# One score fill moved from the long visit to the short one, two gate factors loaded earlier, another deal in the first quad

## The chip, the cores and the metric

The kernel runs on one core of a Trainium2 chip. The metric is the device time of one execution in microseconds; the kernel before took 1105.04 us (median of three runs, 1104.69 to 1105.52). Both kernels compute the same.

## The reference, cut to what matters

The input x has 2048 rows of 640. One branch is causal attention in four segments of 512 rows with 32 heads of 20, mixed per head with a linear memory of the earlier segments; the other is a gated feed-forward layer of width 1728. A gate per row mixes them.

```python
g = sigmoid((x * gate_w).sum(-1, keepdims=True))
for s in range(4):                       # segments of 512 rows
    p = softmax(qs @ ks.T * scale + causal_mask)
    a_dot = p @ vs
    a_mem = (phi(qs) @ M) / (phi(qs) @ z + 1e-6)
    o = sigmoid(beta) * a_mem + (1 - sigmoid(beta)) * a_dot
    M, z = M + phi(ks).T @ vs, z + phi(ks).sum()
a = concat(o) @ wo
b = (silu(x @ w1) * (x @ w3)) @ w2
out = g * a + (1 - g) * b
```

## The kernel before

**Dense work.** The four segments are chunks 0 to 3, in two halves A (chunks 0, 1) and B (2, 3). Every 32-bit operand is split into a rounded part and a rest, and each product is three matmuls. A dense group is one PSUM bank of 128 x 512 that is filled by 15 matmuls (`g` and `u`: the two feed-forward projections; `q`, `k`, `v`; `op`: the output projection) or by 9 or 5 (`f`: the second feed-forward product). DVE or ACT then empties it: a `u` group by one DVE pass (`ft`, L528), a `g` group by an ACT pass and a DVE pass (`ft` L519, `fu` L520), an `f` group by a DVE pass (L588, L550) or, in the first group of a chunk, by an ACT copy (L586). Dense work is a list of generators (`seg`), from which `step` draws some three matmuls at a time.

**Banks.** PSUM has eight banks that `bank_tile` deals in rotation from the list `free`. The bank of an open dense group is held back (`held`) and goes to the end of the list when the group's last matmul is issued (`filled`).

**Attention.** Four heads are a quad `m`; each quad is 40 slots of `attention()`. `s_fill` (scores, scanned on DVE for the row maximum, L641), `t_fill` (transposed scores with the maximum subtracted, exponentiated on ACT, L673, cut to a triangle on POOL, L677) and `pv_quad` (`o`, the product with V, copied by DVE, L691) are issued in two visits per quad: the long one at slot `BIG` (5), the short one at slot `SMALL` (17). Each fill has two tiles, one for each of two heads that PE works side by side on different rows of its array; `o` has one tile. The table `VISITS` gives the order: the long visit holds s fill 0 of quad m, t fills 0 and 1 of quad m-1, o of quad m-2, t fill 3, s fill 2, t fill 2 and s fill 1, 15 tiles in all; the short one s fill 3, t fill 4 and s fill 4, six tiles. The visit of quad 1 is cut in two parts: 3 fills, then 4, and 3 in the short visit. A long visit waits until no dense group is open (at most 8 steps), a short one stands also inside an open group. `load_pair` loads the q and k rows of the next quad behind each visit, through POOL's queue.

**Other tiles of the rotation.** The memory read (`nd`, L352), the normalization of the attention output (`rr` and `gt`, L761 and L766, emptied by DVE at L762 and L767), and the split of an input chunk (`xh`, L131) also take banks. Each chunk's sum is multiplied by its gate factor `sh`, which `load_share` loads through ACT's queue (L740); `finish` and `share` use it (L550, L543).

**Order.** PE runs in the order in which the program issues. The order on the other engines is fixed when the kernel is built, by a planner that places each instruction where its inputs are due; each engine then works strictly in that order.

Of the kernel before, what the change touches and what calls it, by code (L numbers as in the profile page):

```python
# [25 lines left out]
BIG = -1.0e38  # L26
# [12 lines left out]
def gated_mix(ctx: ExitStack, tc: tile.TileContext, xT, wqk, wv, w13, w2, w2h, wo, beta, out):  # L39
# [60 lines left out]


    here = tc.keep_in_program_order
    last = {}

    def split(dst, src, lo=None, pin=lambda ins: ins):
        pin(nc.scalar.copy(dst[:, 0], src))  # L106
# [4 lines left out]
    def bank_tile(name, hold=None):  # L111


        k = free.pop(0)
        ps = pp.tile([P, L], F32, tag=f"b{k}", name=name, bufs=1)
        if hold:
            held[k] = -hold
        else:
            free.append(k)
        return ps  # L120
# [6 lines left out]
    def split_psum(dst, src, name, pin=lambda ins: ins):  # L127

        hi = bank_tile(name)[:, :src.shape[-1]]
        pin(nc.scalar.copy(dst[:, 0], src))  # L130
        nc.scalar.copy(hi, dst[:, 0].bitcast(F32))  # L131
        nc.vector.tensor_sub(dst[:, 1], src, hi)
# [134 lines left out]
    late, stored = [], set()  # L267
# [70 lines left out]
    def memory_read(c):  # L338
        pq = big.pop(("q", c))[:, :KB * L].rearrange("p (b n) -> p b n", b=KB)
        for qb in range(4):  # L340
            for hf in range(2):
                gm = f_tile(f"gm{c}_{qb}_{hf}")[:, :320]
                ps = bank_tile(f"nd{c}_{qb}_{hf}")
                nd = ps[:, :16 * VE].rearrange("p (h e) -> p h e", e=VE)
                todo = []
                for b in range(KB):
                    a0, a1 = HEADS[b]
                    u0, u1 = max(a0, 16 * hf), min(a1, 16 * hf + 15)
                    if u0 <= u1:
                        todo.append((b, a0, u0, u1))  # L350
                for n, (b, a0, u0, u1) in enumerate(todo):
                    nc.tensor.matmul(nd[:, u0 - 16 * hf:u1 - 16 * hf + 1, :],  # L352
                                     pq[:, b, qb * P:(qb + 1) * P],
                                     Ms[c - 1, b][:, u0 - a0:u1 - a0 + 1, :],
                                     start=n == 0, stop=n == len(todo) - 1, skip_group_check=True)
                r = sp.tile([P, 16], F32, tag="r16", name="nd_r")
                nc.vector.scalar_tensor_tensor(r, nd[:, :, DH], 1e-6, gH[:, 16 * hf:16 * hf + 16], op0=ALU.add, op1=ALU.mult)
                nc.vector.reciprocal(r, r)
                nc.vector.scalar_tensor_tensor(
                    gm.rearrange("p (h e) -> p h e", e=DH), nd[:, :, :DH], gate[:, c, 1, qb:qb + 1],  # L360
                    r.unsqueeze(2).broadcast_to([P, 16, DH]), op0=ALU.mult, op1=ALU.mult)
                store_later(gd[c][:, qb, 320 * hf:320 * hf + 320], gm, ("g", c, qb), n=2)
                yield 700
# [200 lines left out]
    def ffn_down(cs, js, idx, last=()):  # L564
        first = js[0] == 0
        w2s = [w_get(i, idx[0]) for i in idx]
        for c in cs:
            if c in last and c < 2:
                load_share(c)
            if first:  # L570
                accs[c] = slot(f"acc{c}")[:, :KB * L].rearrange("p (b n) -> p b n", b=KB)
            for fb in range(KB):
                for n0, n1 in ((0, 256), (256, L)) if last and (c, fb) == (NSEG - 1, KB - 1) else ((0, L),):
                    ps = bank_tile(f"f{c}_{js[0]}_{fb}_{n0}", 1300 if len(js) > 2 else 690)
                    ms = []
                    for j, w in zip(js, w2s):
                        for a, b in (PASSES if j < NF else ((0, 0), (0, 1))):
                            ms.append((w[:, b, fb * P:(fb + 1) * P], hts[c, j][:, a, n0:n1]))
                    for n, (w, h) in enumerate(ms):
                        nc.tensor.matmul(ps[:, :n1 - n0], w, h, start=n == 0, stop=n == len(ms) - 1)  # L580
                        if n % 3 == 2 and n < len(ms) - 1:
                            yield 699.0 if n == 2 and len(ms) > 5 else 699
                    filled()
                    dst = accs[c][:, fb]
                    if first:
                        nc.scalar.copy(dst, ps)  # L586
                    elif c not in last:
                        nc.vector.tensor_add(dst, ps, dst)  # L588
                    elif c < 2:
                        finish(c, fb, ps)  # L590
                    else:
                        finish_shared(c, fb, ps, n0, n1 - n0)
                    yield 699 if len(ms) % 3 == 0 else 466

    def both_shares():
        for c in B:
            load_share(c)
            yield 1

# [138 lines left out]
    def load_share(c):  # L738
        shares[c] = sp.tile([P, L], F32, tag="oq" if c == NSEG - 1 else "share", name=f"sh{c}", bufs=1)
        here(nc.scalar.dma_start(shares[c], ed[c][0].rearrange("a n -> (a n)").unsqueeze(0).broadcast_to([P, L])))  # L740
# [12 lines left out]
    def normalize(c):  # L753

        assert c in turned
        if not c:
            gms[c] = big_tile(f"oT{c}", FR)[:, :KB * L].rearrange("p (b n) -> p b n", b=KB)
        for b in range(KB):
            o, hi = f_tile(f"on{c}_{b}"), gms[c][:, b]
            ps = bank_tile(f"rr{c}_{b}")  # L760
            nc.tensor.matmul(ps, sel[:, b * P:(b + 1) * P], rR, start=True, stop=True)  # L761
            nc.vector.tensor_mul(o, oall[c][:, b].bitcast(F32), ps)  # L762
            if c:
                pt = bank_tile(f"gt{c}_{b}")
                for qb in range(4):
                    nc.tensor.transpose(pt[:, qb * P:(qb + 1) * P], hi[:, qb * P:(qb + 1) * P].bitcast(F32), ident)  # L766
                nc.vector.tensor_add(o, o, pt)  # L767
            nc.scalar.copy(hi, o)
            nc.vector.tensor_sub(oall[c][:, b], o, hi.bitcast(F32))
            yield 700  # L770
# [8 lines left out]
    def tick():  # L779
        for e in list(soon):  # L780
            e[0] -= 1
            if e[0] <= 0:
# [4 lines left out]


    BIG, SMALL = 5, 17
    VISITS = {BIG: (("s", 0, 0), ("t", 1, 0), ("t", 1, 1), ("o", 2), ("t", 1, 3), ("s", 0, 2), ("t", 1, 2), ("s", 0, 1)),  # L790
              SMALL: (("s", 0, 3), ("t", 1, 4), ("s", 0, 4))}

    def attention():

        for m in range(-1, NQUAD + 2):
            for n in range(40):
                if m == -1 and n < 40 - LEAD:
                    continue

                todo = VISITS.get(n, ()) if m != 1 else {BIG: VISITS[BIG][:3], BIG + 6: VISITS[BIG][4:]}.get(n, VISITS.get(n, ()))  # L800
                todo = [(kind, m - q, f) for kind, q, *f in todo if 0 <= m - q < NQUAD]
                if todo:
                    yield "amid" if len(todo) < 4 else "between"
                    for kind, q, f in todo:
                        if kind == "o":
                            pv_quad(2 * q)
                        else:
                            (s_fill if kind == "s" else t_fill)(q, *f)
                    if n == SMALL and 0 <= m < NQUAD:
                        after(4, max_rows, 2 * m)  # L810
                elif n in ((24, 36) if m < 0 else (BIG + (1 if m > 1 else 7), SMALL + 1)) and m + 1 < NQUAD:
                    load_pair(2 * (m + 1) + (n > BIG + 7 if m >= 0 else n > 24))
                tick()
                yield m
# [5 lines left out]
    def oproj(c, plan):  # L820

        ws, oT = [], []

        def first():
            yield from normalize(c)
            oT.extend((gms[c], oall[c]))

        def rest():
            ws.extend(w_get(i, plan[0]) for i in plan)
            if c == 1:  # L830
                load_share(c)
            for fb in range(KB):
                ps = bank_tile(f"op{c}_{fb}", 1300)
                n = 0
# [95 lines left out]
    seg = [d, braid(chain(u), o1, 5), o2] + [job_up(A, j) for j in GROUPS[3][2:]] + [job_down(A, 3)]  # L930
    u0, u1 = jobs_up_by_chunk(A, 4)
    x2, x3 = split_x(2), split_x(3)
    seg += [(0, load_raw(2)), (0, load_raw(3))] + u0 + [braid(chain(u1), (0, x2), 4, 0, False)]
    d = job_down(A, 4, (0,))
    q = job_q(B[:1], 0, {2: big_tile})
    seg += [braid(chain([braid(d, (0, x2), 5)] + q), (0, x3), 4, 10)] + job_v(B)
# [21 lines left out]
    segs.append((NJ + LAG, seg))  # L958
    d, u = job_down(B, 3), jobs_up(B, 4)
    o1, o2 = jobs_oproj(3)  # L960
    tail = [braid(chain([d, (0, both_shares())] + u), o1, 4, 10)] + [braid(o2, (0, shared(2)), 3), job_down(B, 4, B)]

    for n, (_, g) in enumerate(head):
        for _ in g:
# [29 lines left out]
    while run:  # L994
# [6 lines left out]
        place = next(att, None)  # L1001
        if isinstance(place, str):

            for _ in range(4 if place == "amid" else 8):
                if (max(held.values(), default=-1) >= 0) if place == "amid" else not held:
                    break
                d = step(run)
                if d is None:
                    break
                credit -= d  # L1010
            next(att)
# [68 lines left out]
```

## Time and profile before

| what | value |
|---|---|
| median of the runs | 1105.04 us |
| the profiled execution | 1107.25 us, span 1105.4 us |
| PE busy | 1094.9 us (99%) |
| DVE, POOL, ACT busy | 598.1, 584.6, 381.3 us |
| granted clock of PE | 1.00 |

A profile row of the timeline gives the start and length in us, the engine, the line, the operation with its tile names, the count, and in brackets the idle time of the engine before it with what ended it. Matmuls overlap: the next starts before the last one has ended, so the time of a stretch is read from start to start.

### The profile page before, as it was taken

Reading aid. Unit: us, or ns where it says so; the run is one execution under the profiler, and the core shown is the slowest. Engines: PE = TensorE matmul, PEld = TensorE weight load, DVE = VectorE, ACT = ScalarE, POOL = GpSimd, SP = SyncE. Lnnn points to the kernel's source line nnn. Section 1 sums busy time; section 2 is a strip of 40 time slices with the busy share of each in tenths; the row PEclk is TensorE's granted clock in tenths of the full one; section 3 lists DMA queues with packets and bytes.
Section 4 is the critical chain, followed back from the end, with each engine's and each line's share of the span. In section 5 each row is a group of like instructions: output and inputs, shape, how many; then the busy total and the mean of one; then the engine's idle time right before and its main releaser. Section 6 shows DMA issues by size and latency. Waiting matters only on the chain.

```text
span 1105.4 us, 17904 instructions
## 1 busy us (share of the span) xinstructions
PE 1094.9 (99%) x6290; PEld 853.0 (77%) x6290; DVE 598.1 (54%) x1711; ACT 381.3 (34%) x826; POOL 584.6 (53%) x729
## 2 busy tenths in 40 slices
PE   9999999999999999999999999999999999999998
PEld 6988877777777777787977777777777777777787
DVE  5032564356555554366153678875557665651575
ACT  6244233343233122145244543325333332223020
POOL 5055556366366363565066447556774665655263
PEclk9999999999999999999999999999999999999999
DMA  8256943334355134435367966365664343433122
GB/s 306 110 205 220 281 125 82 95 82 116 77 142 129 51 84 123 126 94 171 121 197 265 288 215 183 97 161 146 151 159 109 85 116 96 117 103 89 52 79 95
DMA packets 87545, 153.20 MB, mean 139 GB/s; under 512 B 11584, under 2 KB 25184, under 8 KB 87456
## 3 DMA queue, kind: packets, MB, share of 16 engines
q1 hardware_dynamic: 63040, 106.30, 30.1%
q0 software_dynamic: 20384, 38.68, 15.9%
q10 hardware_dynamic: 4032, 7.08, 1.8%
q8 instruction: 50, 0.82, 0.3%
q14 instruction: 39, 0.32, 0.1%
HBM read 96.56 MB, written 54.54 MB: 137 GB/s over the span
## 4 chain that ended last, share of the span: by engine, by line
PE 93%; DVE 4%; ACT 1%; DMA 1%; issue 1%; ACTq 0%; SPq 0%; DVEq 0%
PE g L257 16%; PE f L580 16%; PE u L257 16%; PE k L257 6%; PE v L385 6%; PE op L837 6%; PE o L687 6%; PE q L257 5%; PE s L634 5%; PE t L667 4%; PE nd L352 1%; PE pm L449 1%; PE q L327 1%; DVE junk L641 1%; DMA sh<-ed 1%
## 5 line engine op out<-in xcount | busy, mean ns | idle before, releaser
L641 DVE CUSTOM_DVE_ANT_0 junk<-s,mask 128x256 bf16<-128x256 f32 (+3 forms) x512 | 250.3, 489 | 105.9 <-PE s L634 73.6
L673 ACT ACTIVATE P<-t 128x512 f32<-128x512 f32 (+1 forms) x384 | 172.5, 536 | 190.2 <-PE t L667 153.0
L257 PE MATMUL g<-X,W 128*128 128x512 f32 x840 | 208.5, 398 | 0.0
L179 POOL TENSOR_TENSOR W<-wr,W 128x640 fp32r<-128x640 f32 (+1 forms) x126 | 198.5, 1581 | 2.5
L174 POOL CAST W<-wr 128x640 fp32r<-128x640 f32 (+1 forms) x126 | 92.5, 739 | 202.0 <-PE f L580 47.7
L580 PE MATMUL f<-ht,W 128*128 128x512 f32 (+1 forms) x825 | 197.0, 395 | 0.7 <-DVE acc L550 0.7
L257 PE MATMUL u<-X,W 128*128 128x512 f32 x780 | 196.7, 399 | 0.0
L677 POOL TENSOR_SCALAR_AFFINE_SELECT P<-P 128x256 f32<-128x256 f32 x192 | 94.6, 502 | 183.2 <-ACT P L673 182.9
L257 PEld LDWEIGHTS g<-X,W 128*128 128x128 f32 x840 | 155.9, 188 | 36.6 <-issue 0.4
L580 PEld LDWEIGHTS f<-ht,W 128*128 128x128 f32 x825 | 152.9, 188 | 37.6 <-DVE acc L550 1.5
L257 PEld LDWEIGHTS u<-X,W 128*128 128x128 f32 x780 | 144.0, 188 | 34.4 <-ACT P L673 0.3
L107 POOL TENSOR_TENSOR ht<-ft,ht 128x512 fp32r<-128x512 f32 x52 | 67.2, 1291 | 90.1 <-ACT ht L106 90.0
L611 POOL DMA_DIRECT2D qk<-qkd x128 | 83.6, 655 | 0.5 <-issue 0.2
L634 PE MATMUL s<-qk 60*128 60x256 f32 (+3 forms) x512 | 77.8, 345 | 1.1 <-DVE fu L520 1.0
L257 PE MATMUL k<-X,W 128*128 128x512 f32 x300 | 77.0, 403 | 0.0
L687 PE MATMUL o<-P,vg 128*32 128x512 f32 (+3 forms) x1024 | 75.5, 435 | 1.4 <-DVE on L767 1.4
L519 ACT ACTIVATE ft<-g 128x512 f32<-128x512 f32 x52 | 31.2, 599 | 124.9 <-PE g L257 113.8
L385 PE MATMUL v<-W,X 128*128 128x320 f32 (+1 forms) x480 | 71.9, 311 | 0.3 <-ACT P L673 0.3
L520 DVE SCALAR_TENSOR_TENSOR fu<-ft,g 128x512 f32<-128x512 f32 x52 | 35.7, 686 | 67.3 <-ACT ft L519 58.3
L385 PEld LDWEIGHTS v<-W,X 128*128 128x128 f32 x480 | 71.0, 189 | 1.0 <-ACT P L673 0.5
L106 ACT CAST ht<-ft 128x512 fp32r<-128x512 f32 x52 | 32.2, 619 | 110.9 <-DVE ft L528 110.8
L588 DVE TENSOR_TENSOR acc<-f,acc 128x512 f32<-128x512 f32 x65 | 44.7, 689 | 44.8 <-PE f L580 44.6
(123 smaller groups left out, 1204.8 us busy)
## 6 DMA issues: line engine op xcount, KB each, us to landing
qk<-qkd POOLq DMA_DIRECT2D x128, 240.0 KB, 4.0
wr<-in_w_dram SPq DMA_DIRECT2D x80, 320.0 KB
qkd<-qs SPq DMA_DIRECT2D x20, 512.0 KB
qkd<-ks SPq DMA_DIRECT2D x20, 512.0 KB
od<-oq SPq DMA_DIRECT2D x32, 256.0 KB
wr<-in_wo_dram SPq DMA_DIRECT2D x20, 320.0 KB
vg<-vd SPq DMA_DIRECT2D x16, 336.0 KB
xr<-in_xT_dram SPq DMA_DIRECT2D x20, 256.0 KB
```

The lines of the kernel that those rows point to most:

```text
L107: (lo or nc.gpsimd.tensor_sub)(dst[:, 1], src, dst[:, 0].bitcast(F32))
L174: hi = nc.gpsimd.tensor_copy(w[:, 0, :n], raw[:, :n])
L179: last["low"] = nc.gpsimd.tensor_sub(w[:, 1, :n], raw[:, :n], w[:, 0, :n].bitcast(F32))
L257: nc.tensor.matmul(ps, w[:, a, kb * P:(kb + 1) * P], x[:, b, kb, :], start=n == 0, stop=n == 14)
L385: nc.tensor.matmul(ps[:, :n1 - n0], x[:, a, kb, lb * P:(lb + 1) * P], wvt[kb][:, b, n0:n1], start=n == 0, stop=n == 14)
L580: nc.tensor.matmul(ps[:, :n1 - n0], w, h, start=n == 0, stop=n == len(ms) - 1)
L611: here(nc.gpsimd.dma_start(t[64 * i:64 * i + RH], qkd[c][RH * (h + i):RH * (h + i + 1)]))
L634: nc.tensor.matmul(ps[i][:, o:o + w], q[:, qb * P:(qb + 1) * P], key[:, :w], start=n == 0, stop=n == len(todo) - 1, skip_group_check=True)
L641: nc.vector.tensor_tensor_reduce(out=junk[:, :w], in0=ps[i][:, o:o + w], in1=mask[:, L - w:], scale=1.0, scalar=-3.0e38, op0=ALU.add, op1= ...
L673: last["exp"] = nc.scalar.activation(pairs[2 * m + k]["P"][:, i, o:o + n], ps[i][:, b:b + n], AF.Exp, scale=SCALE)
L677: nc.gpsimd.affine_select(d, d, pattern=[[0, 2], [0, n], [1, P]], base=0, channel_multiplier=-1, compare_op=ALU.is_ge, fill=0.0)
L687: nc.tensor.matmul(ps[32 * i:32 * i + 32, kb * P:], heads[2 * p + i]["v"][:, kb], pairs[p + i // 2]["P"][:, i % 2, o:o + n], start=kb == 0 ...
```

## The change

- A long visit leaves out t fill 3 of quad m-1 when the dense group that was opened last is a `u`, `f`, `op` or `g` group and more than six steps have passed since a small tile took a bank. Then the short visit of that quad has four fills, t fill 3 first (eight tiles), and does not stand inside an open group: from slot 8 on it is taken as soon as the last group is a finished `u`, `f` or `op` group, at least five steps after the long visit and three after the last small tile. At slot 17 it waits for that for up to eight steps, or until 14 steps have passed since the long visit.
- The visit of quad 1 is cut into 4, 3 and 3 fills.
- The gate factor of chunk 0 is loaded ahead of the last feed-forward unit's up projections instead of inside its down projection; that of chunk 1 at the start of the normalization instead of the output projection.

```diff
     def split_psum(dst, src, name, pin=lambda ins: ins):
+        if src.shape[-1] == L:
+            last["small"] = clock["step"]
...
     def ffn_down(cs, js, idx, last=()):
         for c in cs:
-            if c in last and c < 2:
-                load_share(c)
...
+    PLAIN = "ufo"
     VISITS = {BIG: (("s", 0, 0), ("t", 1, 0), ("t", 1, 1), ("o", 2), ("t", 1, 3), ("s", 0, 2), ("t", 1, 2), ("s", 0, 1)),
-              SMALL: (("s", 0, 3), ("t", 1, 4), ("s", 0, 4))}
+              SMALL: (("s", 0, 3), ("t", 1, 4), ("s", 0, 4)),
+              "four": (("t", 1, 3), ("s", 0, 3), ("t", 1, 4), ("s", 0, 4))}
...
-                todo = VISITS.get(n, ()) if m != 1 else {BIG: VISITS[BIG][:3], BIG + 6: VISITS[BIG][4:]}.get(n, VISITS.get(n, ()))
+                todo = VISITS.get(n, ()) if m != 1 else {BIG: VISITS[BIG][:3] + VISITS[BIG][4:5], BIG + 6: VISITS[BIG][5:]}.get(n, VISITS.get(n, ()))
+                if n == SMALL or four and not done and 8 <= n < SMALL:
+                    if not done and 0 <= m <= NQUAD:
+                        yield "amid" if not four else "late" if n == SMALL else "early"
+                        if n == SMALL or last["go"]:
+                            visit(m, VISITS["four" if four else SMALL])
+                            done = True
...
+                    if ("t", 1, 3) in todo and 0 < m <= NQUAD and last["dense"] in PLAIN + "g" and clock["step"] - last["small"] > 6:
+                        four = True
+                        todo = [t for t in todo if t != ("t", 1, 3)]
...
         def first():
+            if c == 1:
+                load_share(c)
             yield from normalize(c)
         def rest():
             ws.extend(w_get(i, plan[0]) for i in plan)
-            if c == 1:
-                load_share(c)
...
-    seg += [(0, load_raw(2)), (0, load_raw(3))] + u0 + [braid(chain(u1), (0, x2), 4, 0, False)]
+    seg += [(0, load_raw(2)), (0, load_raw(3)), (0, load_shares(A[:1]))] + u0 + [braid(chain(u1), (0, x2), 4, 0, False)]
...
+            def ready():
+                if place == "amid":
+                    return max(held.values(), default=-1) >= 0
+                if place == "between":
+                    return not held
+                return not held and last["dense"] in PLAIN and clock["step"] - last["visit"] >= 5 \
+                    and clock["step"] - last["small"] > 2
+            last["go"] = ready()
-            for _ in range(4 if place == "amid" else 8):
-                if (max(held.values(), default=-1) >= 0) if place == "amid" else not held:
+            for _ in range({"amid": 4, "early": 0}.get(place, 8)):
+                if ready() or place == "late" and clock["step"] - last["visit"] >= 14:
                     break
```

More of the change, by code (lines that the diff above doesn't have):

```diff
@@ L102, in gated_mix @@
     here = tc.keep_in_program_order
-    last = {}
+    last = dict(small=0, visit=0)
     def split(dst, src, lo=None, pin=lambda ins: ins):
@@ L117, in bank_tile @@
             held[k] = -hold
+            last["dense"] = name[0]
         else:
@@ L343, in memory_read @@
                 ps = bank_tile(f"nd{c}_{qb}_{hf}")
+                last["small"] = clock["step"]
                 nd = ps[:, :16 * VE].rearrange("p (h e) -> p h e", e=VE)
@@ L593, in ffn_down, with load_shares @@
                     yield 699 if len(ms) % 3 == 0 else 466
-    def both_shares():
-        for c in B:
+    def load_shares(cs):
+        for c in cs:
             load_share(c)
@@ L760, in normalize @@
             ps = bank_tile(f"rr{c}_{b}")
+            last["small"] = clock["step"]
             nc.tensor.matmul(ps, sel[:, b * P:(b + 1) * P], rR, start=True, stop=True)
@@ L789, in gated_mix, with visit @@
     BIG, SMALL = 5, 17
+    PLAIN = "ufo"
     VISITS = {BIG: (("s", 0, 0), ("t", 1, 0), ("t", 1, 1), ("o", 2), ("t", 1, 3), ("s", 0, 2), ("t", 1, 2), ("s", 0, 1)),
-              SMALL: (("s", 0, 3), ("t", 1, 4), ("s", 0, 4))}
+              SMALL: (("s", 0, 3), ("t", 1, 4), ("s", 0, 4)),
+              "four": (("t", 1, 3), ("s", 0, 3), ("t", 1, 4), ("s", 0, 4))}
     def attention():
+        def visit(m, todo):
+            for kind, q, *f in todo:
+                if 0 <= m - q < NQUAD:
+                    if kind == "o":
+                        pv_quad(2 * (m - q))
+                    else:
+                        (s_fill if kind == "s" else t_fill)(m - q, *f)
         for m in range(-1, NQUAD + 2):
+            four = done = False
             for n in range(40):
@@ L798, in attention @@
                     continue
-                todo = VISITS.get(n, ()) if m != 1 else {BIG: VISITS[BIG][:3], BIG + 6: VISITS[BIG][4:]}.get(n, VISITS.get(n, ()))
[L801 to L811, printed above, removed]
+                todo = VISITS.get(n, ()) if m != 1 else {BIG: VISITS[BIG][:3] + VISITS[BIG][4:5], BIG + 6: VISITS[BIG][5:]}.get(n, VISITS.get(n, ()))
+                n_fills = sum(0 <= m - q < NQUAD for _, q, *_ in todo)
+                if n == SMALL or four and not done and 8 <= n < SMALL:
[4 more added lines that the diff above has]
+                            done = True
+                            if m < NQUAD:
+                                after(4, max_rows, 2 * m)
+                elif n_fills:
+                    yield "amid" if n_fills < 4 else "between"
+                    if ("t", 1, 3) in todo and 0 < m <= NQUAD and last["dense"] in PLAIN + "g" and clock["step"] - last["small"] > 6:
+                        four = True
+                        todo = [t for t in todo if t != ("t", 1, 3)]
+                    visit(m, todo)
+                    last["visit"] = clock["step"]
+                if n in ((24, 36) if m < 0 else (BIG + (1 if m > 1 else 7), SMALL + 1)) and m + 1 < NQUAD:
                     load_pair(2 * (m + 1) + (n > BIG + 7 if m >= 0 else n > 24))
@@ L960, in gated_mix @@
     o1, o2 = jobs_oproj(3)
-    tail = [braid(chain([d, (0, both_shares())] + u), o1, 4, 10)] + [braid(o2, (0, shared(2)), 3), job_down(B, 4, B)]
+    tail = [braid(chain([d, (0, load_shares(B))] + u), o1, 4, 10)] + [braid(o2, (0, shared(2)), 3), job_down(B, 4, B)]
     for n, (_, g) in enumerate(head):
```

## The prediction

> **What bounds the kernel now.** I read the page first, then the waits of PE, then the timeline at the places where a wait ended late.
>
> ```profile
> span 1105.4 us, 17904 instructions
> PE 1094.9 (99%) x6290; PEld 853.0 (77%) x6290; DVE 598.1 (54%) x1711; ACT 381.3 (34%) x826; POOL 584.6 (53%) x729
> PE 93%; DVE 4%; ACT 1%; DMA 1%; issue 1%; ACTq 0%; SPq 0%; DVEq 0%
> PE o L687 <- DVE on L767: 1.4, 1, 1.4
> ```
>
> PE is busy for 99% of the span and carries 93% of the chain. The change adds and removes no matmul, so it can only move waits and slow restarts of PE. The last row is the longest wait that PE shows as idle time (total, times, longest); others are hidden inside busy time. The timeline of one quad shows such a one, in columns of start, length, engine, line, operation, count and idle time before:
>
> ```profile
> 318.44 0.50 PE L634 MATMUL s<-qk 60*128 60x512 f32 x2
> 318.78 0.64 PE L667 MATMUL t<-qk 62*128 62x512 f32 x6
> 319.35 2.36 PE L687 MATMUL o<-P,vg 128*32 128x512 f32 x32
> 321.64 0.50 PE L667 MATMUL t<-qk 62*128 62x512 f32 x2
> 321.78 0.69 DVE L691 COPY oq<-o 128x512 f32<-128x512 f32 x1 [0.90 <-PE o L687]
> 321.98 0.40 PE L634 MATMUL s<-qk 60*128 60x512 f32 x2
> 322.21 0.40 PE L667 MATMUL t<-qk 62*128 62x256 f32 x4
> 322.23 2.19 ACT L673 ACTIVATE P<-t 128x512 f32<-128x512 f32 x6 [0.90 <-PE t L667]
> 322.45 0.58 PE L634 MATMUL s<-qk 60*128 60x384 f32 x4
> 322.95 3.77 PE L257 MATMUL u<-X,W 128*128 128x512 f32 x15
> 326.56 1.54 PE L257 MATMUL g<-X,W 128*128 128x512 f32 x6
> 326.76 0.69 DVE L528 SCALAR_TENSOR_TENSOR ft<-fu,u 128x512 f32<-128x512 f32 x1 [0.73 <-PE u L257]
> 328.04 0.51 PE L634 MATMUL s<-qk 60*128 60x256 f32 x4
> 328.38 0.41 PE L667 MATMUL t<-qk 62*128 62x384 f32 x4
> 328.61 0.46 PE L634 MATMUL s<-qk 60*128 60x384 f32 x4
> 329.00 0.96 PE L257 MATMUL g<-X,W 128*128 128x512 f32 x3
> ```
>
> From start to start the long visit takes 4.51 us (318.44 to 322.95), the short one 0.96. A fill of one 512 pair takes 0.34 when it comes first after another kind of work (321.64 to 321.98, 318.44 to 318.78) and 0.23 behind its like (321.98 to 322.21): about 0.10 goes to the switch. The pairs of 384 and 128 take 0.23 as a t fill (328.38 to 328.61); before dense work, 0.10 more, so 0.33. The long visit's last s fill has the same pairs and takes 0.50. It is the 14th and 15th tile on eight banks: the 15th has the bank of o, which DVE copies until 322.47. A matmul starts 0.05 after such a release (below: 154.67 and 154.72), so the second head starts at 322.52 instead of 322.45. A wait of 0.07 costs 0.17, since the two heads no longer run side by side.
>
> **The change part by part.** Term C, the moved fill. On PE, in the long visit of an earlier quad (o is the product with V, t_3 the moved fill, s_2 the next fill; _0 and _1 are the two heads, the last number is a tile's own), before:
>
> ```order
> L687 MATMUL o_2291<-P_2050,vg_93 32x128 x2
> L667 MATMUL t_3_0_2311<-qk_91 128x512
> L667 MATMUL t_3_1_2312<-qk_91 128x512
> L634 MATMUL s_2_0_2319<-qk_90 128x512
> L634 MATMUL s_2_1_2320<-qk_90 128x512
> ```
>
> and in the same quad's short visit of the changed kernel, behind the u group:
>
> ```order
> L260 MATMUL u_3_2369<-X_105,W_1933 128x512 x15
> L669 MATMUL t_3_0_2393<-qk_91 128x512
> L669 MATMUL t_3_1_2394<-qk_91 128x512
> L636 MATMUL s_3_0_2400<-qk_90 128x256
> L636 MATMUL s_3_1_2401<-qk_90 128x256
> ```
>
> The fill now follows a finished u group instead of o. Switches stay as many: s now pays the 0.10 behind o, t pays it behind u, s_3 no longer. The long visit has 13 tiles, so none reuses o's bank: 0.17 saved. By the order this holds for 21 quads with such a last s fill: 21 x 0.17 = 3.57.
>
> The short visit pays. It has eight tiles, and the eighth has the bank of the group just finished. A u group is released 0.73 after its modelled end (322.95 + 3.77 = 326.72; DVE ends at 327.45), plus 0.05; a visit starts 0.08 before that end. So the bank is free 0.86 after the visit's start, wanted at 0.34 + 0.24 + 0.23 = 0.81. That wait of 0.05 costs up to 0.15 with the lost pairing. The next group also takes t_3's bank: the first exponential starts 0.59 after its fill (321.64, 322.23), an ACT pass takes 0.59 (next row), free at 1.23 where 1.20 is wanted: 0.03 at least.
>
> ```profile
> L586 ACT COPY acc<-f 128x512 f32<-128x512 f32 x20 | 11.7, 588 | 23.2 <-PE f L580 18.9 <-DMA qk<-mr 2.2 <-issue 1.7
> ```
>
> Between 0.03 and 0.15 I take 0.09, for 18 visits: 1.62. Two visits follow an f group that ACT copies itself; the exponential then starts late: about 0.15 each, 0.30. One visit (t_3 of quad 11) stands inside an open group, which leaves seven banks: its last tile waits for t_3's own bank (1.23 instead of 0.81), with the pairing 0.5. C = 3.57 - 1.62 - 0.30 - 0.5 = 1.15 gained, between 0.1 and 1.9.
>
> The Trainium skill, TensorEngine Tiling (Array Packing), section Tiling Modes, says that tiles operate independently and load weights and multiply in parallel. By it a late head would cost only its wait, C would be 21 x 0.07 - 18 x 0.05 - 0.8 = -0.2, and the time 1101.4. The trace disagrees: 0.50 against 0.33 for a wait of 0.07.
>
> With the fill go its two exponentials on ACT and one triangle select on POOL, and POOL issues the next pair's loads behind that select:
>
> ```profile
> qk<-qkd POOLq DMA_DIRECT2D x128, 240.0 KB, 4.0
> ```
>
> They land 4.0 us after issue. Until the next long visit's s_2, which needs them, lie at least two dense groups (3.6 each, as 322.95 to 326.56) and 3.5 us of that visit (318.44 to 321.98), 10.7 in all. I cost this at nothing; where the cover is gone, each us late is a us of PE.
>
> Term A, the factor of the first chunk. On ACT before (X and xh: the split of the next input):
>
> ```order
> L130 CAST X_4932<-xr_4776 128x512
> L131 COPY xh_1_4961<-X_4932 128x512
> L131 COPY xh_2_4983<-X_4932 128x512
> L106 CAST ht_12_4971<-ft_12_4972 128x512
> L740 DMA sh_4999<-ed_84 128x512
> ```
>
> and now:
>
> ```order
> L675 ACTIVATE P_4733<-t_2_0_4729 128x256
> L675 ACTIVATE P_4686<-t_2_1_4730 128x256
> L675 ACTIVATE P_4733<-t_2_1_4730 128x256
> L742 DMA sh_4783<-ed_84 128x512
> L535 ACTIVATE ft_13_4812<-g_13_4785 64x512
> ```
>
> The load has moved up by a whole unit, to behind the exponentials of the long visit near 470 us. What it stands in now:
>
> ```profile
> 496.37 0.32 ACTq L740 DMA_DIRECT2D sh<-ed  x1
> 499.76 5.01 PE L580 MATMUL f<-ht,W 128*128 128x512 f32 x21
> 503.12 1.29 DVE L543 TENSOR_TENSOR acc<-acc,sh 128x512 f32<-128x512 f32 x2 [3.35 <-DMA sh<-ed]
> 505.07 1.44 PE L580 MATMUL f<-ht,W 128*128 128x512 f32 x5 [0.30 <-DVE acc L550]
> 506.87 1.43 PE L580 MATMUL f<-ht,W 128*128 128x512 f32 x5 [0.35 <-DVE acc L550]
> 508.67 3.74 PE L257 MATMUL q<-X,W 128*128 128x512 f32 x15 [0.36 <-DVE acc L588]
> 512.34 0.51 PE L634 MATMUL s<-qk 60*128 60x512 f32 x2
> 517.85 2.33 PE L385 MATMUL v<-W,X 128*128 128x320 f32 x14 [0.30 <-ACT P L673]
> ```
>
> Issued at 496.37, it lands near 503; DVE stands 3.35 us with all accumulations queued behind. PE needs 8.91 us (499.76 to 508.67) for 31 matmuls; at the pace of 322.95 to 326.56 (3.61 for 15 with one switch, 0.234 each) it would be 7.25: 1.66 lost. The visit at 512.34 takes 5.51 instead of 4.51: 1.00 more. What is late next is DVE itself: per group of five matmuls (1.17 us) it owes three passes of about 0.64 (1.29 for two), so it still falls behind by 0.7 a group, but the banks cover four groups. I keep 0.2 at the visit: A = 2.45, between 1.0 and 2.66. The issue costs ACT's queue 0.32 under a dense group.
>
> Term B, the second chunk's normalization (rr and gt: its two banks per block). On DVE the order changes from
>
> ```order
> L762 TENSOR_TENSOR on_2_7298<-oall_6264,rr_2_7299 128x512
> L528 SCALAR_TENSOR_TENSOR ft_2_7269<-fu_2_7270,u_2_7273 128x512
> L641 ISA junk,m_7138<-s_0_0_7316,mask 128x512
> L641 ISA m_7138 128x1
> L767 TENSOR_TENSOR on_2_7298<-on_2_7298,gt_2_7302 128x512
> ```
>
> to
>
> ```order
> L765 TENSOR_TENSOR on_2_7300<-oall_6264,rr_2_7301 128x512
> L772 TENSOR_TENSOR oall_6264<-on_1_7279,gm_6764 128x512
> L770 TENSOR_TENSOR on_2_7300<-on_2_7300,gt_2_7304 128x512
> L532 SCALAR_TENSOR_TENSOR ft_2_7271<-fu_2_7272,u_2_7275 128x512
> L643 ISA junk,m_7131<-s_0_0_7318,mask 128x512
> ```
>
> The pass that frees gt_2's bank moves ahead of the u group's and of the first scan. It matters here:
>
> ```profile
> 696.52 1.07 ACTq L655 DMA_DIRECT2D qk<-mr  x2
> 698.45 0.69 DVE L769 TENSOR_TENSOR oall<-on,gm 128x512 fp32r<-128x512 f32 x1 [1.24 <-ACT gm L768]
> 701.33 0.50 PE L634 MATMUL s<-qk 60*128 60x512 f32 x2
> 702.85 0.68 DVE L767 TENSOR_TENSOR on<-on,gt 128x512 f32<-128x512 f32 x1
> 703.68 2.36 PE L687 MATMUL o<-P,vg 128*32 128x512 f32 x32 [1.38 <-DVE on L767]
> 707.40 1.66 PE L257 MATMUL g<-X,W 128*128 128x512 f32 x6
> ```
>
> o waits 1.38 for that pass; the visit takes 6.07, 1.56 too long. DVE had stood 1.24 because ACT issued DMAs first. Now the first cast precedes those issues, but the short visit ahead comes nine matmuls (2.1 us) later and its scans press on the same stretch, and the second factor's load adds 0.32 to ACT. I take 1.0, between -0.5 and 1.56. The second load itself gains nothing: no wait for it is in the trace.
>
> Term D, the first quad's deal of 4, 3, 3:
>
> ```profile
> 152.60 0.50 PE L667 MATMUL t<-qk 62*128 62x512 f32 x2
> 153.99 0.68 DVE L520 SCALAR_TENSOR_TENSOR fu<-ft,g 128x512 f32<-128x512 f32 x1
> 154.72 0.50 PE L634 MATMUL s<-qk 60*128 60x384 f32 x3 [0.98 <-DVE fu L520]
> 155.16 0.95 PE L352 MATMUL nd<-Ms,pq 128*128 128x147 f32 x6
> ```
>
> An eight-tile visit directly behind a g group takes 2.56 where 0.34 + 0.23 + 0.24 + 0.33 = 1.14 is due: 1.42 lost. With six tiles there it goes. But the visit before has eight now, behind a u group whose pass is queued after the memory read's; the following g takes a bank that awaits a scan, and the last s waits for six exponentials. From passes of 0.6 to 0.7 I estimate 1.0 lost there: 0.4 gained, between -0.4 and 1.2.
>
> Sum: 2.45 + 1.0 + 1.15 + 0.4 = 5.0. The profiled execution took 1107.25 (span 1105.4) and would take 1102.2; the median before, 1105.04, lies 2.21 below it: 1100.0.
>
> **The rivals.** Slower: the short visit waits for its eighth bank as the visit at 152.60 did, in all 21 places, if DVE has scans ahead of the group's pass. Price up to 1.42 each, 30 against 7.4 of other gains: about 1127. It decides from 0.46 per visit on. Against it: DVE's order has the u pass ahead of the visit's scans. Chance 0.06.
>
> The bank wait only moves: the short visit pays 0.2, C = 3.57 - 3.6 - 0.8 = -0.8: 1102.0. For it: 0.81 and 0.86 are close. Chance 0.2. The Trainium skill's section Performance Considerations, same page, warns that tiling does not speed up the emptying of PSUM; the oq row agrees.
>
> The normalization stays late (B = -0.5): 1101.5. Chance 0.12.
>
> The earlier load does nothing, because DVE's three passes per group bound that stretch anyway (A = 0.5): 1102.0. Chance 0.06.
>
> **How the numbers follow.** The forecast has 0.56. All best ends together give 1097.7, all worst 1104.8; eight in ten lie within 1097.9 to 1103.2. A measurement can tell about 0.2% (2.2 us) from no change: faster, below 1102.83, 0.87; same 0.07; slower 0.06.
>
> **What would show it.** Right: long visits of 4.10 without t_3, short ones of 1.2 to 1.3, no DVE wait on sh, f groups at pace around 500, no o wait near 700. Wrong: short visits above 1.4, or idle rows at s behind a u group.

## The result, and the profile after

The changed kernel took 1108.97 us (median, 1106.99 to 1109.85) against 1104.93 for the kernel before in the same rounds: a ratio of 1.003 (95% interval 1.002 to 1.004), 4 us slower, where 5 us faster was forecast. The first lines of its page, and the waits of PE (total, times, longest):

```profile
span 1105.3 us, 17927 instructions
PE 1093.4 (99%) x6290; PEld 851.7 (77%) x6290; DVE 601.8 (54%) x1711; ACT 379.9 (34%) x826; POOL 584.0 (53%) x729
PE 92%; DVE 3%; ACT 2%; DMA 1%; issue 1%; POOL 0%; SPq 0%; DVEq 0%; POOLq 0%
PE g L260 <- ACT P L675: 2.4, 7, 0.5
PE t L669 <- DVE m L643: 1.6, 1, 1.6
PE t L669 <- DMA qk<-mr: 0.5, 1, 0.5
PE f L582 <- ACT P L675: 0.5, 1, 0.5
PE o L689 <- DVE on L770: 0.2, 1, 0.2
```

The long wait of o for the normalization is nearly gone (0.2 instead of 1.4). New are seven waits of a g group and one of an f group for an exponential, one of 1.6 for a scan, one of 0.5 for the row maxima.

This span is as short as that of the profiled execution of before (1105.4), though the timed medians are 4 us apart: each of the two executions was unlike most others of its kernel. A second profile of each puts it right: 1103.2 for before, 1107.2 for the changed kernel, 3.92 apart. The accounts below use that second pair, matmul against the same matmul.

**The moved fill.** Two short visits of the changed kernel on the timeline, the first as forecast:

```profile
178.21 0.50 PE L669 MATMUL t<-qk 62*128 62x512 f32 x2
178.74 1.09 ACT L675 ACTIVATE P<-t 128x512 f32<-128x512 f32 x2 [3.13 <-PE t L669]
179.03 0.53 PE L636 MATMUL s<-qk 60*128 60x384 f32 x4
179.48 3.73 PE L260 MATMUL g<-X,W 128*128 128x512 f32 x15
...
232.11 0.50 PE L669 MATMUL t<-qk 62*128 62x512 f32 x2
232.65 1.08 ACT L675 ACTIVATE P<-t 128x512 f32<-128x512 f32 x2 [3.30 <-PE t L669]
232.93 0.53 PE L636 MATMUL s<-qk 60*128 60x384 f32 x4
233.78 3.50 PE L260 MATMUL g<-X,W 128*128 128x512 f32 x14 [0.33 <-ACT P L675]
```

The first lasts 1.27 (178.21 to 179.48), the second 1.67: there the group behind starts only when both exponentials have ended (233.73). Which bank it has is told by the order in which the tiles take their banks in the built program (tile and bank; t1_3_0 is fill t_3 of quad 1, first head; nh is the small tile, 16 columns wide, that splits the row maxima of the next quad):

```
first visit:   t1_3_0:1 t1_3_1:6 s2_3_0:0 s2_3_1:7 t1_4_0:4 t1_4_1:2 s2_4_0:3 s2_4_1:5 g1_2:1 nh4:6
second visit:  t3_3_0:4 t3_3_1:2 s4_3_0:3 s4_3_1:5 t3_4_0:6 t3_4_1:1 s4_4_0:0 s4_4_1:7 nh8:4 g0_4:2
```

In the first, the group takes the bank of t_3's first head; in the second, nh takes that bank, and the group gets the second head's, which is free one ACT pass later.

**The 1.6.** The visit of quad 9 near 386, in the changed kernel:

```profile
384.28 1.31 POOL L613 DMA_DIRECT2D qk<-qkd  x2 [0.47 <-issue]
384.99 2.73 DVE L772 TENSOR_TENSOR oall<-on,oT 128x512 fp32r<-128x512 f32 x1
385.61 1.56 POOL L182 TENSOR_TENSOR W<-wr,W 128x640 fp32r<-128x640 f32 x1
386.10 0.51 PE L669 MATMUL t<-qk 62*128 62x512 f32 x2
387.65 0.55 DVE L643 CUSTOM_DVE_ANT_0 junk<-s,mask 128x384 bf16<-128x384 f32 x1
388.59 0.44 PE L669 MATMUL t<-qk 62*128 62x384 f32 x2 [1.59 <-DVE m L643]
```

A DVE pass that takes 0.69 elsewhere takes 2.73 here, beside POOL's weight split. It starts 0.62 ahead of the split, while POOL still issues loads, and ends 0.55 behind it; whether the issuing holds it up too, no run separates. Behind it stand the scans of s_1's second head from the long visit, whose bank t_4 of this visit is to have. And in the second profile the wait, 1.57 there, had a sequel. Its windows, and then one of the first profile, show the busy time of PE, its weight loads, DVE, ACT and POOL, then the granted clock, third from the end:

```profile
388.97 0.44 PE L669 MATMUL t<-qk 62*128 62x384 f32 x2 [1.57 <-DVE m L643]
388.00:390.00 2.00, 0.98 (x8) 0.60 (x8) 1.93 (x9) 0.56 (x2) 0.42 (x1) 1.00 0.60 171
390.00:394.00 4.00, 4.00 (x13) 3.19 (x12) 3.75 (x15) 1.77 (x4) 2.25 (x3) 0.57 0.00 0
394.00:404.00 10.00, 10.00 (x45) 7.62 (x44) 6.03 (x14) 3.30 (x7) 6.39 (x7) 1.00 0.16 50
```

```profile
390.00:394.00 4.00, 4.00 (x19) 3.08 (x18) 3.62 (x14) 1.81 (x4) 2.58 (x4) 1.00 0.00 0
```

A mean of 0.57 over 4 us is half speed for about 3.4 us (4 x (1 - 0.57) / 0.5). The matmuls came 0.43 apart instead of 0.23, and the g group behind took 5.23 instead of 3.67: 1.56 us were lost. Ten of eleven timed runs of the changed kernel show a mean clock of 0.998, as such a fall would give (3.4 x 0.5 of 1107 us is 0.0015); the one that the first profile shows had 1.000 and is the fastest. The mean does not tell where the clock fell: in the profile of the last experiment below, also 0.998, it read 0.63 and 0.52 in the windows from 7 to 11 us, at the start. Only the second profile shows the fall at quad 9.

### The profile page after: what moved, and what is told of

It reads as the page before. It is cut to its first block, busy times and chain, and to the rows that moved or that the text cites. A ratio compares the mean times of both kernels' runs of the same rounds, so it can differ in the third digit from the quotient of the medians.

```text
span 1105.3 us, 17927 instructions
## 1 busy us (share of the span) xinstructions
PE 1093.4 (99%) x6290; PEld 851.7 (77%) x6290; DVE 601.8 (54%) x1711; ACT 379.9 (34%) x826; POOL 584.0 (53%) x729
## 4 chain that ended last, share of the span: by engine, by line
PE 92%; DVE 3%; ACT 2%; DMA 1%; issue 1%; POOL 0%; SPq 0%; DVEq 0%; POOLq 0%
PE g L260 18%; PE f L582 16%; PE u L260 16%; PE v L389 6%; PE k L260 6%; PE op L857 6%; PE o L689 6%; PE q L260 5%; PE s L636 4%; PE t L669 3%; PE nd L356 1%; PE pm L453 1%; PE q L330 1%; ACT P L675 1%; DVE junk L643 1%
## 5 line engine op out<-in xcount | busy, mean ns | idle before, releaser
L260 PE MATMUL u<-X,W 128*128 128x512 f32 x780 | 194.1, 398 | 0.0
L679 POOL TENSOR_SCALAR_AFFINE_SELECT P<-P 128x256 f32<-128x256 f32 (+1 forms) x192 | 92.9, 493 | 191.4 <-ACT P L675 191.2
L532 DVE SCALAR_TENSOR_TENSOR ft<-fu,u 128x512 f32<-128x512 f32 x52 | 35.7, 687 | 59.9 <-PE u L260 59.6
```

Source lines behind the costliest of these rows:

```text
L260: nc.tensor.matmul(ps, w[:, a, kb * P:(kb + 1) * P], x[:, b, kb, :], start=n == 0, stop=n == 14)
L679: nc.gpsimd.affine_select(d, d, pattern=[[0, 2], [0, n], [1, P]], base=0, channel_multiplier=-1, compare_op=ALU.is_ge, fill=0.0)
```

## The experiments

**Both kernels again.** No edit.

> The changed kernel once more, unaltered. The profiled execution of it took 1106.99 and that of before 1107.25, but the timed medians stand 4.0 apart (1108.97 and 1104.93). Theory 1 (the moved fill costs what the trace shows, about 4.5, and the three other terms give about 4.1 back): the kernel is near no change in a profile, and the 4 us of the timed runs are a matter of the single runs (clock 0.998 in five of six); then the spread between runs should show again, with times between 1105 and 1109. Rival (a steady cost that only undisturbed timed runs show): five rounds again near 1109 and a ratio of 1.003 to 1.004, with a profiled execution that is faster than the timed ones.

> The kernel before, unaltered, as its own control: ratio 1.000 within 0.001, time near 1105. Its clock and span in each run are wanted: if they read 1.000 and near 1103 where the changed kernel has 0.998 and near 1107, the clock accounts for 2 of the 4 us; if they read 0.998 too, the clock tells nothing. Its profiled execution shows by how much two traces of one kernel differ (the start of the first q group differed by 0.5 us between the two that are there).

The changed kernel: 1108.88, ratio 1.0034 (1.0022 to 1.0046), clock 0.998 in all five runs. Before: 1105.11, ratio 1.0002, clock 1.000 or 0.999 in ten of eleven. So the 4 us are steady, the rival's case, and neither first profile was typical. What the first profile of before had and the second lacks is the late factor. The second profile of before:

```profile
DVE acc L543 <- DMA sh<-ed: 1.1, 1, 1.1
500.99 1.29 DVE L543 TENSOR_TENSOR acc<-acc,sh 128x512 f32<-128x512 f32 x2 [1.06 <-DMA sh<-ed]
510.96 0.88 PE L667 MATMUL t<-qk 62*128 62x512 f32 x6
```

The factor landed by 501 instead of 503; DVE stood 1.06 instead of 3.35, and PE was 2.25 us earlier by the end of the visit that follows. That is the whole distance of the first profile to its median (2.21).

**Without the moved fill.**

```diff
-                    if ("t", 1, 3) in todo and 0 < m <= NQUAD and ...
+                    if False and ("t", 1, 3) in todo and 0 < m <= NQUAD and ...
```

> The changed kernel without the moved fill: every long visit keeps its 15 tiles; the two earlier loads and the deal of 4, 3, 3 stay. Theory 1: the trace shows -1.7 at the f groups near 500, -1.3 at the normalization near 700 and -1.1 in the first quad, so 1100.8, ratio 0.996. Rival (the loss is not in the visits but in what the earlier loads do to DMA or clock): near 1109 as the changed kernel, at any rate above 1105.

1103.65, ratio 0.9986 (0.9978 to 0.9995): the loss sits in the moved fill, as theory 1 has it, but the other terms give 1.5, not 4.1: the 1.7 at the f groups had been read against the first profile of before, with its late factor. Against the second profile of before they are: first quad -1.06, normalization -0.71, the factor of chunk 0 **+0.57**. That last one was to be the largest gain. In this kernel's timeline:

```profile
497.32 0.72 POOL L177 CAST W<-wr 128x642 fp32r<-128x642 f32 x1
497.53 3.05 DVE L547 TENSOR_TENSOR acc<-acc,sh 128x512 f32<-128x512 f32 x2
498.12 1.91 POOL L182 TENSOR_TENSOR W<-wr,W 128x642 fp32r<-128x642 f32 x1
503.49 0.67 DVE L547 TENSOR_TENSOR acc<-acc,sh 128x512 f32<-128x512 f32 x1
509.84 1.47 PE L669 MATMUL t<-qk 62*128 62x512 f32 x6
```

The first two products take 3.05 together (1.06 and 2.06) beside POOL's weight split, its cast and its subtraction; the third takes 0.67 without it. DVE is behind for the rest of the stretch, and the t fills of the visit stretch from 0.88 to 1.47.

**nh behind the next group.**

```diff
     def max_rows(p):
+        if not held:
+            after(1, max_rows, p)
+            return
```

> The changed kernel, with the small tile nh (split of the row maxima) put off until a dense group is open. In the trace of the changed kernel the visits with four fills lose 0.09 to 0.1 where the next dense group opens ahead of nh (it has the bank of t_3_0), and 0.4 to 0.55 more where nh takes that bank first and the group gets the bank of t_3_1. Theory 1: about twelve such places, 12 x 0.42 = 5.0 less, so about 1104 and a ratio near 0.999; the dense group behind a visit starts 0.15 after the last fill everywhere but at the visit at 386. Rival (the wait only moves, to nh on ACT or to the group after): within 1 us of the changed kernel.

1106.42, ratio 1.001 (1.0001 to 1.0019), 2.5 less than the changed kernel instead of 5. The mechanism is as said, the count was not: eight places, not twelve, and all eight waits are gone (0.4 to 0.5 each, 3.3 in all). The visit that was at 232.11, in this kernel:

```profile
232.70 0.50 PE L672 MATMUL t<-qk 62*128 62x512 f32 x2
233.51 0.54 PE L636 MATMUL s<-qk 60*128 60x384 f32 x4
233.98 3.28 PE L260 MATMUL g<-X,W 128*128 128x512 f32 x13
```

1.28 instead of 1.67. Elsewhere 1.1 came back: the wait for the row maxima near 786 grew from 0.52 to 1.14, that of o near 702 from 0.16 to 0.59. So the traces give 2.2 for this edit; the 2.5 between the medians holds the clock too. The twelve runs part by it: five at 1104.97 to 1105.91 read 1.000, four at 1106.42 to 1106.61 read 0.998, three at 1108.52 to 1109.07 read 0.997. The wait of 1.6 at quad 9 is still in this kernel, and in its profile, one of the five, the clock stayed up.

**Quad 9 left alone.** The condition above gets `and m != 10`.

> The changed kernel, with fill t_3 of quad 9 left in its long visit (the short visit near 386 us goes back to three fills); all else as in the changed kernel. Theory (a wait that sets off the clock): near 387 us PE stands 1.6 us for a bank that a scan on DVE releases, and in the slower of the two traces of the changed kernel the granted clock then falls to 0.76 for about 4 us, 1.6 us more. Without that visit both go: about 1108.9 - 3.3 = 1105.6, and the clock reads 1.000 or 0.999 in most runs instead of 0.998. Rival (the clock falls for another reason, as under the load of the DMAs): the wait goes, the clock stays at 0.998, about 1107.2.

1106.22, ratio 1.0007 (0.9998 to 1.0016), 2.7 less than the changed kernel and 0.6 above the 1105.6; the clock reads 1.000 or 0.999 in ten of eleven runs. The low mean clock goes with the wait: the rival falls.

**The slow DVE pass moved to POOL.**

```diff
-            nc.vector.tensor_sub(oall[c][:, b], o, hi.bitcast(F32))
+            (nc.vector if c else nc.gpsimd).tensor_sub(oall[c][:, b], o, hi.bitcast(F32))
```

> The changed kernel, with the last step of chunk 0's normalization (remainder = on - oT, two operands in SBUF) on POOL instead of DVE, five passes. Theory: at 385 us this pass takes 2.73 us on DVE instead of 0.69, because POOL runs its weight split beside it; two scans of s_1 stand behind it, and the short visit of quad 9 needs their banks. With the pass on POOL's own queue the scans go on, the wait of 1.6 at 387 shrinks to 0.3 or less, the clock no longer falls: 1108.9 - 3.0 = about 1106, clock 1.000 in most runs. Rival (the visit simply stands too close, 3.5 us, behind the long one, and DVE is too far behind in any case): the wait stays above 1, about 1108 to 1109.

1107.41, ratio 1.0013 (1.0004 to 1.0022), between the forecast and its rival. The timeline of quad 9's visit, which still stands 3.5 behind the long one, and a wait of PE:

```profile
386.28 1.31 POOL L772 TENSOR_TENSOR oall<-on,oT 128x512 fp32r<-128x512 f32 x1
387.08 0.51 PE L669 MATMUL t<-qk 62*128 62x512 f32 x2
387.66 0.41 PE L669 MATMUL t<-qk 62*128 62x384 f32 x4
PE op L857 <- POOL W L182: 1.3, 1, 1.3
```

t_4 follows without a wait and the clock stays at 1.000 in most runs, so the wait came from the pass of 2.73 and not from the visit's place. 1.3 of the gain is given back at 415, where a weight that POOL now splits later is late for PE.

**The factor of chunk 0 in its old place**, without the moved fill:

```diff
+            if c in last and c < 2:
+                load_share(c)
...
-    seg += [(0, load_raw(2)), (0, load_raw(3)), (0, load_shares(A[:1]))] + u0 + ...
+    seg += [(0, load_raw(2)), (0, load_raw(3))] + u0 + ...
```

> No moved fill, and the factor of chunk 0 loaded where before loaded it; left of the change are the earlier factor of chunk 1 and the deal of 4, 3, 3. Theory: the early factor of chunk 0 is a loss of 0.57 in an ordinary execution. With the factor there in time, DVE starts its two products of accumulator and factor while POOL splits a weight, and they take 1.06 and 2.07 us instead of 0.68; with the load in its old place they fall behind POOL's work. So 0.5 to 0.6 less than the kernel without the moved fill (1103.65): 1103.1, and both products at 0.68. Rival, as predicted before (the early factor saves 1.0 to 2.6): 1104.7 to 1106.3, with the same state of the first quad and the normalization.

The time does not confirm it: 1104.03, ratio 0.9988 (0.9979 to 0.9997), no different from the kernel with the early load (1103.65). The trace does:

```profile
499.53 1.29 DVE L547 TENSOR_TENSOR acc<-acc,sh 128x512 f32<-128x512 f32 x2 [1.02 <-DMA sh<-ed]
509.55 0.82 PE L671 MATMUL t<-qk 62*128 62x512 f32 x6
```

The two products take 1.29 together, and the visit at 509.21 lasts 5.13 instead of 5.70. The runs lie in two groups, five at 1102.9 to 1103.4 and six at 1104.0 to 1105.3. A factor that lands late in some of them, as in the first profile of before, would do this; their traces are not there, so it stays open.

**The gains together**: `m not in (10, 12, 22)`, nh behind the group, the factor of chunk 0 in its old place; and the same with the early factor.

> The parts that the traces show as gains put together: the moved fill without quads 9, 11 and 21, the tile nh put off until a dense group is open, the earlier factor of chunk 1, the deal of 4, 3, 3, and the factor of chunk 0 in its old place. Theory: 1105.1 - 1.06 (first quad) - 0.71 (normalization) - 18 x 0.08 (moved fills) = 1101.9, ratio 0.997. Rival (the gain of 0.08 per quad is given back at the next wait, as in the long visit that waits for the row maxima at 785): as the kernel without the moved fill, 1103.1 or more.

> As the kernel that puts the gains together, but with the factor of chunk 0 loaded early, as the change has it. Theory (DVE's two products meet POOL's weight split): 0.57 slower than that kernel, 1102.4; the two products near 500 us take 1.06 and 2.07. Rival (the early load gains): 1100 to 1101.

1102.16, ratio 0.9973 (0.9964 to 0.9982), and 1102.80, ratio 0.9980 (0.9972 to 0.9989), in rounds side by side, against 1101.9 and 1102.4 expected. They are 0.64 apart where 0.57 was expected, though the intervals overlap; in the two traces the stretch around 510 makes 0.58. Against the trace of the kernel before this pair the moved fill now gains 0.04 to 0.12 in 14 of the 19 quads where it still moves, and loses 0.27 at quad 23.

**Two products on POOL**, with the early factor; and then one more quad left alone (`m not in (10, 12, 22, 24)`).

```diff
-        i = (nc.gpsimd if c == 2 or c == 1 and fb % 2 == 0 else nc.vector).tensor_mul(d, d, shares[c])
+        i = (nc.gpsimd if c == 2 or c == 0 and fb < 2 or c == 1 and fb % 2 == 0 else nc.vector).tensor_mul(d, d, shares[c])
```

> The kernel that puts the gains together, with the early factor of chunk 0, and with the first two products of accumulator and factor on POOL instead of DVE (behind its weight split there). Theory (contention of a DVE pass with two operands in SBUF and POOL): the two products no longer hold DVE for 3.05 us, the third fill of the visit near 510 no longer waits 0.57: 1102.8 - 0.6 = 1102.2, and no dependence on when the factor lands. Rival (DVE is bound there by its number of passes, or POOL hands the accumulators on too late): the visit still loses 0.5, about 1102.8 or more.

> As the kernel with the two products on POOL, and in addition t_3 of quad 23 left in its long visit (its move lost 0.3 to 0.65 near 812 us in the two kernels that put the gains together). Theory: 0.3 to 0.6 below that kernel, about 1101.8, the fastest of all. Rival: the loss turns up at the next quad, no change.

1101.97, ratio 0.9964 (0.9951 to 0.9976), and 1102.00, ratio 0.9965 (0.9953 to 0.9978), from five runs each. The first is the lowest median of all, but its interval overlaps those of 1102.16 and 1102.80. In its trace:

```profile
496.06 2.55 POOL L547 TENSOR_TENSOR acc<-acc,sh 128x512 f32<-128x512 f32 x2
498.64 1.19 DVE L547 TENSOR_TENSOR acc<-acc,sh 128x512 f32<-128x512 f32 x1
508.56 0.63 PE L672 MATMUL t<-qk 62*128 62x512 f32 x6
```

The t fills are at their pace (0.63) and the 0.57 is gone: against the trace of the kernel with the early factor the visit gains 0.84, of which 0.28 is given back by 557. The quad left alone changes nothing that can be measured.

## Why the prediction was wrong

| term | predicted gain | measured, second profiles |
|---|---|---|
| A, factor of chunk 0 | 2.45 | -0.57 |
| B, normalization | 1.0 | 1.36 (0.71 without the moved fill) |
| D, first quad | 0.4 | 1.06 |
| C, moved fill | 1.15 | -6.1 |
| sum | 5.0 | -4.25 (the two traces differ by 3.92) |

Of the 0.33 that the sum leaves, 0.32 is a gain near 888, in the third chunk's normalization, which shows only with the moved fill and which no term has.

**A: an outlier was priced as the rule.** The prediction subtracted 2.21 as a uniform distance of the profiled execution from the median and then booked 2.45 as a gain against the same execution. The distance was that stall. In the second profile of before PE runs the f groups at pace (50 matmuls in 11.52, 495.54 to 507.06) and the visit behind them takes 5.14, as in the kernels without a stall there (5.13), so there was nothing to win. The step "What is late next is DVE itself", with 0.2 kept for it at the visit, was also short: DVE took 3.05 for two products and the visit lost 0.57. The price stood in the trace of before, in groups kept apart by shape and in its last stage:

```profile
L769 DVE TENSOR_TENSOR oall<-on,gm 128x512 fp32r<-128x512 f32 x15 | 13.6, 909 | 3.3 <-ACT gm L768 3.3
L762 DVE TENSOR_TENSOR on<-oall,rr 128x512 f32<-128x512 f32 x20 | 13.6, 679 | 0.0
1076.90 4.25 POOL L543 TENSOR_TENSOR acc<-acc,sh 128x512 f32<-128x512 f32 x3
1076.92 1.82 DVE L543 TENSOR_TENSOR acc<-acc,sh 128x512 f32<-128x512 f32 x1
```

The first two are passes of one shape; the one with both operands in SBUF takes 909 ns on average, the one with an operand in PSUM 679. And the product of a later chunk with its factor, from the same line as this term's, took 1.82 beside POOL.

**B and D** went the forecast way, D at 1.06 inside its bounds. B comes to 1.36, but 0.65 of it shows only with the moved fill, from whose later short visit the prediction expected pressure on this stretch; why it helps stays open. Alone, B is 0.71 of the 1.0. The eight-tile visit lost less than the estimate of 1.0: it stands at 146.62 in the changed kernel and loses 0.5.

**C: the parts on PE held, the bank behind them did not.** The long visit without t_3 takes 4.10 (forecast 4.10), the good short visit 1.27 (1.2 to 1.3); a quad with a good visit gains 0.05 to 0.11 where 0.17 - 0.09 = 0.08 was worked out. The step that failed is "The next group also takes t_3's bank", with "free at 1.23 where 1.20 is wanted: 0.03 at least". It left out that nh can take a bank of the same rotation between the visit and the group. The change does keep its short visits away from small tiles, but `split_psum` notes only tiles of full width (`src.shape[-1] == L`), so nh with its 16 columns is not among the tiles that it steers clear of. Against the kernel without the moved fill, C's 6.1 are: seven quads where nh comes first, 2.2; quad 9, 3.25 (1.6 of wait, 1.56 of clock); the quads around 787, 1.1 (0.52 for the row maxima, the rest nh and lost pairing); quad 11, 0.24 (inside the open group, 0.5 - 0.17 forecast); twelve good ones, -0.7.

Two more steps fell. "I cost this at nothing", of what goes with the fill, followed the q and k rows to the next long visit, but the first t fill of the next long visit waits for the row maxima, whose chain of scans, nh and DMA starts one fill later (where nh was put off further still, this wait grew to 1.14):

```profile
786.00 0.73 PE L669 MATMUL t<-qk 62*128 62x512 f32 x6 [0.52 <-DMA qk<-mr]
```

And the slower rival was held too small at 0.06 because its mechanism, scans ahead of what frees the bank, was asked of the u group alone. As it was put, a wait for the eighth bank in all 21 places, it did not come true. A wait like it came in one visit of 22, at quad 9, for the sixth tile, whose bank awaited a scan while DVE had the normalization as well. There it cost 3.25, the clock included.

The Trainium skill, TensorEngine Tiling (Array Packing), section Tiling Modes, says that tiles operate independently; the reading of it that a late head costs only its wait (0.07) does not hold here. The saving of 0.40 per long visit (0.23 of the fill and 0.17) was found as worked out from the trace.

## What to carry to other kernels

Where a profiled execution stands 2 us off the median of its kernel, look for those 2 us in its trace before pricing any stall of that size; a second profile settles it. When tiles are dealt from a rotation, write out the bank of every tile behind a moved piece, the small tiles of other engines' work included: one 16-column tile decided 0.4 us in eight places. Before a wait is taken away, look which engine runs at the moment the work will then start.

## What the runs showed of the hardware

A DVE pass of 128x512 that reads two operands from SBUF is held up by POOL's arithmetic: 0.68 alone; 1.06, 2.06 and 2.73 beside POOL's weight split; 1.3 beside its other two-operand pass. Passes with an operand in PSUM kept 0.67 to 0.69 beside the same work in all rows. The held passes whose rows are shown ended about 0.55 after the POOL instruction did (500.58 after 500.03, 387.72 after 387.17), as if they were held until POOL was through. POOL's split took 1.91 instead of 1.58 when a DVE product ran into its start. The Trainium skill, GPSIMD Engine Reference, section Specifications, says that GpSimd shares its SBUF interfaces with VectorE and contends with instructions of two SBUF inputs; the rows agree and add the price.

Behind a pause of 1.57 us within a visit PE's clock fell to half for about 3.4 us (0.57 over 4 us) in one of the two profiles of the changed kernel, and not in the other, nor in that of the kernel with nh put off, which has the same pause. The mean clocks of the timed runs fit a fall in most executions with the pause and in few without it: 0.998 or 0.997 in 17 of 23 runs of the two kernels that have it, in 2 of 22 of the two experiments that take it away. The Trainium skill, TensorE: Matmul & The Clock Gate, section What's actually happening, puts the fall behind an idle window of about 3.4 us that runs free of the program; the length of the fall and its coming and going agree, but here no pause was that long. What sets it off stays open. With 1.56 us lost, the clock cost as much as the wait ahead of it.
